# Landmark attention, gated MLP and mish MLP on one core: a new order of steps, other buffers for batch 1, larger weight DMAs

## The chip, the cores and the metric

The kernel runs on one core of a Trainium2 chip. The metric is the device time of one execution in microseconds (us), the median of several runs. In the text PE is TensorE (matrix products, with weight loads, PEld, beside them), DVE is VectorE, ACT is ScalarE, POOL is GpSimd and SP is SyncE, whose queue issues every DMA. PSUM is the memory of 8 banks that PE writes to, SBUF the working memory.

## The reference

Three stages follow each other. With q, k and v of 4 batches, 8 heads, 576 positions and 64 channels:

```python
q_lm = q.reshape(B, H, 32, 18, D).mean(axis=3)
k_lm = k.reshape(B, H, 32, 18, D).mean(axis=3)
A, Bm, C = sm(q, k_lm), sm(q_lm, k_lm), sm(q_lm, k)
Z = Bm.T / (norm(Bm, 1) * norm(Bm, inf) + 1e-06)
for _ in range(6):
    Z = 2 * Z - Z @ Bm @ Z
x = A @ Z @ C @ v                      # 2304 tokens x 512
x = ((x @ w1) * (x @ w2) @ w3) @ w_out # 512 -> 1024 -> 1024 -> 512
h = x @ w_in                           # 512 -> 2048
out = (h * tanh(softplus(h))) @ w_out2 # 2048 -> 512
```

`sm` is a softmax of scaled scores. The weights arrive as 64-bit floats.

## The kernel before

**Order.** The program is a set of named steps, each on one engine, with the steps that must come before it; `ORDER` is a list that says in which order they are issued, written out by hand as one string. Every engine works through its own steps strictly in that order, and `@ACT`, `@POOL` or `@DVE` behind a step picks an engine where there is a choice. A step waits by semaphores for the steps it depends on and for the buffer it takes. Buffers come from small pools and go back when their last reader is done.

**Steps.** In the names, the last figures are batch and the like.
- Weights: `ld` (SP, load a unit of 64-bit words), `da` (L201 on ACT, L203 on DVE), `dm` (L207, DVE), `ds` (L210, ACT) and `db` (L214, DVE) decode a unit to 32 bits in four passes. Units are wo0 to wo7 (w_out), w30 to w315 (w3), wBSC (w1 and w2 for batch pair B, slice S, half C) and x0 on (last stage). `hi` and `lo` split a decoded unit in two parts for the three products of `mm3` (L189 to L191).
- w3 @ w_out: `mm n i` (L356), four for each of the 16 units of w3, two PE instructions each; `ehi` and `elo` bring the sums out. The product is computed once, so that the second and third product of the gated MLP become one.
- Attention of a batch: loads `lk`, `lq`, `lv`; landmark sums `ks`, `qs` (DVE for batch 0, five steps on POOL for the others, L417 to L423); their blocks `bdk`, `bdq`; `as`, `amx`, `asb`, `aex`, `asm`, `aad`, `arc`, `amul`, `atr`, `ahi`, `alo` for A; `cs`, `cm`, `cex`, `cad`, `crc`, `ctr`, `cev`, `cv`, `cve` for C @ v; `bs` to `bp` and `ns` to `npy` for Bm and its norms; six rounds `nm` (PE, L646) and `nu` (DVE, L703) for Z; `lt` and `lte` for Z @ C @ v.
- Landmark products: `m b s` (L850) multiplies Z @ C @ v by slice s of w1 and w2; `mh` and `ml` split the result. `xa` and `xb` multiply it by A, `xc` copies one factor, `xm` (L886) multiplies the two into `hslice`.
- `sh` and `sl` split these, `y` multiplies them by the product of w3 and w_out, `ye` brings it out. Behind the list stands the last stage (`p2`), which is not changed.

**Buffers.** w3 and w_out units are decoded in seven raw buffers, four of the pool `raw` and three of `raw2` (`raw_pool`, L327). The latter lie in the memory of M0 to M2, which the landmark products use later; so `m` waits for `mm 15 3`, the last product of w3 and w_out (`add_m`, L842). q and k of batch 1 lie in W0 and W1 (L242), where w1 and w2 are put later, so the last decode step of their first units waits for batch 1's attention (`add_w12`, L816). H0 to H3 hold the results of `xm` (L240). Of the PSUM banks, two are pool `w`, five `pa` (attention) and one `pb`; the step `widen` (L995) moves two from `pa` to `w` after `mm 15 3`.

Of the kernel before, what the change touches and what calls it, by code (L numbers as in the profile page):

```python
# [7 lines left out]
F32 = mybir.dt.float32  # L8
# [14 lines left out]

ORDER = (
# [127 lines left out]
def kernel(  # L152
# [31 lines left out]
    def words(ap):  # L184
        r, n = ap.shape
        return ap.bitcast(I32).rearrange("r (n w) -> r n w", w=2)

    def mm3(o, lh, ll, rh, rl, first, last):
        T.matmul(out=o, lhsT=lh, rhs=rh, start=first, stop=False)  # L189
        T.matmul(out=o, lhsT=lh, rhs=rl, start=False, stop=False)  # L190
# [55 lines left out]
    M = {}  # L246
# [923 lines left out]
```

## Time and profile before

| | us |
|---|---|
| median of 3 runs (776.62 to 778.1) | 777.49 |
| the profiled execution | 776.88 |
| its span, first to last instruction | 775.1 |
| PE busy in the span | 750.3 |
| DVE busy | 350.4 |
| ACT busy | 337.6 |
| POOL busy | 120.1 |

The profile is of one execution. Busy time of an engine is the time in which one of its instructions ran; matmuls are pipelined, so the mean duration of one can be above the distance between two. An instruction's idle time is that of its engine just before it, with the engine and instruction that ended it. The granted clock is a share of TensorE's full speed.

### The profile page before, as it was taken

Reading aid. Unit: us, or ns where it says so; the run is one execution under the profiler, and the core shown is the slowest. Engines: PE = TensorE matmul, PEld = TensorE weight load, DVE = VectorE, ACT = ScalarE, POOL = GpSimd, SP = SyncE. Lnnn points to the kernel's source line nnn. Section 1 sums busy time; section 2 is a strip of 40 time slices with the busy share of each in tenths; the row PEclk is TensorE's granted clock in tenths of the full one; section 3 lists DMA queues with packets and bytes.
Section 4 is the critical chain, followed back from the end, with each engine's and each line's share of the span. In section 5 each row is a group of like instructions: output and inputs, shape, how many; then the busy total and the mean of one; then the engine's idle time right before and its main releaser. Section 6 shows DMA issues by size and latency. Waiting matters only on the chain.

```text
span 775.1 us, 13036 instructions
## 1 busy us (share of the span) xinstructions
PE 750.3 (97%) x5188; PEld 616.3 (80%) x5188; DVE 350.4 (45%) x706; ACT 337.6 (44%) x737; POOL 120.1 (15%) x120
## 2 busy tenths in 40 slices
PE   6887999999999999999999999999999999999997
PEld 2644457888889889999988888888888888888896
DVE  5878868887886663755165122111111112111111
ACT  5456556666664464876443332222222222222222
POOL 0428100520062413231133200000000000000000
PEclk9989899999999999999999999999999999999999
DMA  8993265742332313434130001000100001000100
GB/s 312 369 329 106 80 192 167 256 127 83 117 114 72 110 55 98 140 117 137 30 107 28 1 0 55 1 0 1 55 0 1 1 0 55 1 0 1 55 1 27
DMA packets 38381, 65.92 MB, mean 85 GB/s; under 512 B 3888, under 2 KB 20400, under 8 KB 38320
## 3 DMA queue, kind: packets, MB, share of 16 engines
q1 hardware_dynamic: 38320, 65.09, 25.3%
q8 instruction: 40, 0.66, 0.3%
q14 instruction: 21, 0.17, 0.1%
HBM read 60.36 MB, written 4.72 MB: 84 GB/s over the span
## 4 chain that ended last, share of the span: by engine, by line
PE 91%; DVE 5%; DMA 2%; issue 1%; ACT 1%; POOL 0%; SPq 0%; DVEq 0%; POOLq 0%
PE ps L189 26%; PE ps L191 26%; PE ps L190 26%; PE ps L356 6%; PE ps L850 2%; PE ps L450 1%; DVE raw L207 1%; DMA raw<-in_wo_dram 1%; PE ps L646 1%; DVE raw L214 1%; PE ps L528 1%; PE ps L587 1%; DMA k<-in_kT_dram 1%; PE ps L566 1%; PE ps L506 0%
## 5 line engine op out<-in xcount | busy, mean ns | idle before, releaser
L1101 ACT ACTIVATE emx<-ps 128x512 f32<-128x512 f32 (+1 forms) x80 | 44.3, 554 | 131.6 <-PE ps L191 131.6
L1103 DVE TENSOR_TENSOR gx<-emx,gx 128x512 fp32r<-128x512 f32 (+1 forms) x40 | 25.6, 639 | 158.6 <-ACT gx L1102 158.6
L189 PE MATMUL ps<-hs,W 128*128 128x288 f32 (+2 forms) x304 | 92.7, 305 | 0.0
L190 PE MATMUL ps<-hs,W 128*128 128x288 f32 (+2 forms) x304 | 92.4, 304 | 0.0
L191 PE MATMUL ps<-hs,W 128*128 128x288 f32 (+2 forms) x304 | 92.2, 303 | 0.0
L207 DVE TENSOR_SCALAR raw<-raw 128x512 uint16<-128x512 uint16 x84 | 74.4, 917 | 37.6 <-ACT raw L201 37.2
L1103 DVE TENSOR_TENSOR hs<-emx,hs 128x512 fp32r<-128x512 f32 (+1 forms) x40 | 25.6, 639 | 136.6 <-ACT hs L1102 136.6
L189 PE MATMUL ps<-AT,M 128*128 128x288 f32 x256 | 78.3, 306 | 1.0 <-DVE M L223 0.9
L190 PE MATMUL ps<-AT,M 128*128 128x288 f32 x256 | 75.6, 295 | 0.0
L191 PE MATMUL ps<-AT,M 128*128 128x288 f32 x256 | 75.5, 295 | 0.0
L210 ACT ACTIVATE raw<-raw 128x512 f32<-128x512 f32 x84 | 55.8, 678 | 29.8 <-DVE raw L207 25.6
L356 PE MATMUL ps<-wo,raw 128*128 128x512 f32 x128 | 61.9, 643 | 5.7 <-DVE raw L214 5.7
L201 ACT ACTIVATE raw<-raw 128x512 int32<-128x512 uint16 x79 | 52.7, 673 | 24.2 <-DMA raw<-in_w_dram 10.5
L190 PEld LDWEIGHTS ps<-hs,W 128*128 128x128 f32 x304 | 57.5, 189 | 1.4
L189 PEld LDWEIGHTS ps<-hs,W 128*128 128x128 f32 x304 | 57.1, 188 | 1.8 <-ACT y L218 0.4
L191 PEld LDWEIGHTS ps<-hs,W 128*128 128x128 f32 x304 | 57.5, 189 | 1.2
L356 PEld LDWEIGHTS ps<-wo,raw 128*128 128x128 f32 x128 | 26.6, 212 | 38.2 <-issue 28.6
L189 PEld LDWEIGHTS ps<-AT,M 128*128 128x128 f32 x256 | 48.1, 188 | 8.2 <-issue 2.1
L1102 ACT ACTIVATE gx<-ps 128x512 fp32r<-128x512 f32 (+1 forms) x40 | 22.2, 556 | 61.2 <-PE ps L190 61.2
L190 PEld LDWEIGHTS ps<-AT,M 128*128 128x128 f32 x256 | 48.1, 188 | 0.0
L191 PEld LDWEIGHTS ps<-AT,M 128*128 128x128 f32 x256 | 48.1, 188 | 0.0
L1102 ACT ACTIVATE hs<-ps 128x512 fp32r<-128x512 f32 (+1 forms) x40 | 22.3, 557 | 54.7 <-PE ps L190 54.7
(219 smaller groups left out, 1652.0 us busy)
## 6 DMA issues: line engine op xcount, KB each, us to landing
raw<-in_w_dram SPq DMA_DIRECT2D x128, 128.0 KB, 2.6
raw<-in_wo_dram SPq DMA_DIRECT2D x22, 512.0 KB, 4.4
raw<-in_w3T_dram SPq DMA_DIRECT2D x32, 256.0 KB, 6.5
raw<-in_wi_dram SPq DMA_DIRECT2D x14, 512.0 KB, 3.9
k<-in_kT_dram SPq DMA_DIRECT2D x8, 576.0 KB, 8.3
q<-in_qT_dram SPq DMA_DIRECT2D x8, 576.0 KB, 9.2
out_dram<-osb SPq DMA_DIRECT2D x18, 256.0 KB, 3.4
vt<-in_v_dram SPq DMA_DIRECT2D x4, 1024.0 KB, 7.5
```

What stands on the lines that cost most here:

```text
L189: T.matmul(out=o, lhsT=lh, rhs=rh, start=first, stop=False)
L190: T.matmul(out=o, lhsT=lh, rhs=rl, start=False, stop=False)
L191: T.matmul(out=o, lhsT=ll, rhs=rh, start=False, stop=last)
L201: S.activation(w[..., 0], q[..., 1], ACTF.Copy, scale=2.0 ** -13, bias=2.0 ** -14 - 0.5)
L207: V.tensor_scalar(q[..., 1], q[..., 3], 0x8000, None, op0=ALU.bitwise_and)
L210: S.activation(f32(w[..., 1]), f32(w[..., 1]), ACTF.Copy, scale=2.0 ** -112)
L214: V.scalar_tensor_tensor(to, w[..., 1], 3, w[..., 0], op0=ALU.logical_shift_left, op1=ALU.bitwise_or)
L356: T.matmul(out=got(f"acc{i}"), lhsT=f32(got(f"w3{n}")[:, o:o + 128, 0]), rhs=WO0[j // 4][:, j % 4], start=j == 0, stop=j == 7)
L850: T.matmul(out=got(f"p{c}{key}")[32 * i:32 * i + 32, 0:256], lhsT=LT[r, b, 2 * c + par, :], rhs=w12(f"w{bp}{s}{c}")[r, par * 256:par * 256 ...
L1101: S.activation(x, zt[n], ACTF.Mish)
L1102: S.activation(gb(n, 0), zt.pop(n), ACTF.Mish)
L1103: V.tensor_tensor(gb(n, 1), x, f32(gb(n, 0)), op=ALU.subtract)
```

## The change

- The order is new from the eighth step on. Batch 0's q comes ahead of its k; batch 1's tensors come after more weights; the rounds of Z of batch 0 come after `mm 7`; batch 2's attention starts ahead of `mm 11`; `widen` comes ahead of `mm 9 1`, `m 0 0` ahead of `mm 15 3`. 16 `da` (w100 to w171) go to DVE and that of wo6 to ACT, `lo` of the last stage's units to DVE in place of POOL, `bdk` and `bdq` of batches 2 and 3 to POOL, six more `sl` to POOL.
- Only four units (the 3rd, 5th, 7th and 10th loaded: w30, wo3, wo4, wo6) use `raw2`; `m` waits for these to be read, in place of `mm 15 3`.
- `widen` waits for `lte1 0` and `alo2 0`, in place of `mm 15 3`.
- q and k of batch 1 lie in H2 and H3, in place of W0 and W1, and H0 to H3 are taken when `xm` first writes them. The decoding of w1 and w2 no longer waits for batch 1's attention.
- A w3 unit is loaded by one DMA in place of two, a unit of w1 and w2 by two in place of four.

```diff
+RAW_M = (3, 5, 7, 10)
...
-    "ld wo0,ld wo1,ld w30,ld wo2,ld wo3,ld w31,ld wo4,lk0 0,lq0 0,lk1 0,lq1 0,lv 0,lk0 1,lq0 1,lk1 1,lq1 1,"
-    "da wo0@ACT,dm wo0,da wo1@ACT,ds wo0,dm wo1,db wo0,ds wo1,da w30@ACT,ld wo5,db wo1,dm w30,da wo2@ACT,ld w32,"
...
-    "as2 1,ks3 2,alo2 0,ks4 2,bmx 1,bsb 1,cs0 1,elo 2,da w314@ACT,qs0 2,elo 3,by 1,bdk0 2@ACT,mm 8 0,bdk1 2@ACT,"
...
+    "ld wo0,ld wo1,ld w30,ld wo2,ld wo3,ld w31,ld wo4,lq0 0,lq1 0,da wo0@ACT,dm wo0,lk0 0,da wo1@ACT,ds wo0,"
+    "dm wo1,db wo0,ds wo1,ld wo5,da w30@ACT,db wo1,dm w30,ld w32,da wo2@ACT,ds w30,dm wo2,lk1 0,da wo3@ACT,db w30,"
...
+    "amul2 0,mm 7 0,ld w310,asm1 1,da w39@ACT,mm 7 1,db w38,npy0 0,mm 7 2,npy1 0,dm w39,mm 7 3,ehi 2,aad0 1,"
+    "arc0 1,ks1 2,ds w39,nm0 0,elo 2,ld w311,cs0 1,da w310@ACT,nu0 0,db w39,ehi 3,mm 8 0,cm00 1,ks2 2,cm10 1,"
...
+    "cv1 1,bsm 1,lte1 0,crc1 1,widen,mm 9 1,bad 1,cve1 1,lv 2,brc 1,qs3 2,da w312@ACT,bml 1,mm 9 2,btr 1,qs4 2,"
...
+    "da w010@ACT,ld w020,m 0 0,dm w010,ehi 6,mm 15 3,mh0 0 0,ks0 3,elo 6,mh1 0 0,atr0 2,ds w010,ml0 0 0,ld w021,"
...
+    "ld w041,asb0 3,da w031@ACT,xm 1 0 0,m 1 1,amx1 3,aex0 3,xa 0 1 0,xm 1 0 1,mh0 1 1,atr1 2,mh1 1 1,asm0 3,"
...
+    def words2(ap):
+        return ap.bitcast(I32).rearrange("(a r) (n w) -> r a n w", a=2, w=2)
...
-    HP = [kept(f"H{i}", [128, NS, HALF], F32, f"h{i}") for i in range(4)]
-    QK1 = {x: kept(f"W{i}", [128, NP, S_LEN], F32, f"{x}1") for i, x in enumerate("qk")}
+    HP = {}
+    QK1 = {x: kept(f"H{i + 2}", [128, NP, S_LEN], F32, f"{x}1") for i, x in enumerate("qk")}
...
-        return "raw2" if len(first) % 7 in (0, 3, 5) else "raw"
+        return "raw2" if len(first) in RAW_M else "raw"
...
-            for a in range(2):
-                nc.sync.dma_start(out=r[:, a * 256:(a + 1) * 256, :],
-                                  in_=words(w3T[r0 + a * 128:r0 + a * 128 + 128, c]))
+            nc.sync.dma_start(out=r.rearrange("p (a n) w -> p a n w", a=2), in_=words2(w3T[r0:r0 + 256, c]))
...
-                for p in range(2):
-                    r0 = (2 * c + p) * 128
-                    nc.sync.dma_start(out=r[:, p, i * 128:(i + 1) * 128, :], in_=words(w[r0:r0 + 128, cols]))
-        after = [f"{x} 1" for x in ("qs4", "as0", "as1", "as2", "ks4", "cs0", "cs1")] if bp == 0 else []
+                nc.sync.dma_start(out=r[:, :, i * 128:(i + 1) * 128, :], in_=words2(w[c * 256:(c + 1) * 256, cols]))
...
-             + ["mm 15 3"] + chain("m", key), mm, {"p0" + key: "w", "p1" + key: "w", key: "M"},
+             + vacated + chain("m", key), mm, {"p0" + key: "w", "p1" + key: "w", key: "M"},
...
+        if u % 4 not in HP:
+            HP[u % 4] = kept(f"H{u % 4}", [128, NS, HALF], F32, f"h{u % 4}")
...
-    step("widen", "none", ["mm 15 3"], lambda e: None, {f"w{i}": "pa" for i in range(2)})
+    in_m = [first[i - 1] for i in RAW_M]
+    vacated = [f"db {u}" for u in in_m] + [f"mm {u[2:]} {i}" for u in in_m if u[1] == "3" for i in range(4)]
+    step("widen", "none", ["lte1 0", "alo2 0"], lambda e: None, {f"w{i}": "pa" for i in range(2)})
```

## Rows read from the trace of the kernel before

**Rows 1.** Busy time by stage of the span (x counts instructions).

```profile
core 0: us, PE busy (x) PEld busy (x) DVE busy (x) ACT busy (x) POOL busy (x), PEclk, DMA share, GB/s
0.00:13.48 13.48, 7.41 (x20) 2.54 (x21) 5.17 (x8) 6.27 (x9) 1.26 (x8) 1.00 0.81 277
13.48:22.32 8.84, 8.84 (x18) 3.98 (x19) 8.48 (x11) 4.66 (x11) 0.00 (x0) 0.81 1.06 382
22.32:43.07 20.75, 13.94 (x267) 10.81 (x266) 18.43 (x44) 10.65 (x30) 11.10 (x9) 0.88 1.05 375
43.07:54.83 11.76, 11.76 (x41) 6.01 (x41) 7.86 (x16) 6.56 (x14) 0.00 (x0) 0.78 1.05 357
54.83:80.06 25.23, 20.34 (x84) 11.26 (x83) 22.59 (x32) 15.12 (x32) 17.96 (x14) 0.91 0.33 101
80.06:110.57 30.51, 30.51 (x93) 13.67 (x96) 20.82 (x55) 14.36 (x31) 2.66 (x3) 0.96 0.44 135
110.57:118.55 7.98, 6.97 (x209) 5.24 (x211) 6.77 (x17) 6.74 (x17) 0.00 (x0) 1.00 0.47 148
118.55:240.00 121.45, 119.26 (x1511) 101.35 (x1508) 96.68 (x242) 76.48 (x198) 32.10 (x39) 1.00 0.45 141
240.00:378.00 138.00, 138.00 (x1144) 132.22 (x1143) 79.24 (x153) 83.38 (x184) 36.54 (x36) 1.00 0.30 100
```

**Rows 2.** Waits of PE, longest in total: us, times, longest.

```profile
PE ps L356 <- DVE raw L214: 5.7, 2, 4.6
PE ps L450 <- DVE AT L223: 4.9, 1, 4.9
PE ps L587 <- ACT et L577: 3.4, 1, 3.4
```

**Rows 3.** Chain of work that ended last, 60 to 120 us: start, length.

```profile
66.85 4.56 DVE raw L207 x3
...
80.13 15.12 PE ps L356 x32
...
96.63 13.94 PE ps L356 x32
```

**Rows 4.** Groups on DVE, 80 to 110 us: busy us, mean ns, idle before.

```profile
L207 DVE TENSOR_SCALAR raw<-raw 128x512 uint16<-128x512 uint16 x7 | 5.2, 742 | 5.4 <-ACT raw L201 5.2
...
L214 DVE SCALAR_TENSOR_TENSOR raw<-raw 128x512 int32<-128x512 int32 x4 | 2.7, 683 | 0.0
```

**Rows 5.** Groups on DVE, 0 to 120 us.

```profile
L223 DVE TENSOR_TENSOR W<-ps,W 128x512 fp32r<-128x512 f32 x8 | 5.4, 687 | 5.5 <-ACT W L218 5.4
...
L537 DVE TENSOR_REDUCE cmx<-ps 128x1 f32<-128x288 f32 x8 | 3.4, 449 | 0.3 <-PE ps L528 0.3
...
L703 DVE SCALAR_TENSOR_TENSOR py<-py,ps 128x128 f32<-128x128 f32 x10 | 2.9, 288 | 1.8 <-PE ps L646 1.7
...
L459 DVE TENSOR_REDUCE mx<-ps 128x16 f32<-128x512 f32 x4 | 2.7, 687 | 0.9 <-PE ps L450 0.9
...
L203 DVE TENSOR_SCALAR raw<-raw 128x512 uint16<-128x512 uint16 x1 | 1.2, 1246 | 0.0
```

**Rows 6.** Groups on DVE, 62 to 77 us.

```profile
L207 DVE TENSOR_SCALAR raw<-raw 128x512 uint16<-128x512 uint16 x6 | 8.0, 1428 | 2.3 <-ACT raw L201 2.3
L214 DVE SCALAR_TENSOR_TENSOR raw<-raw 128x512 int32<-128x512 int32 x5 | 6.7, 1379 | 0.0
```

**Rows 7.** Group of L646 on PE, whole span.

```profile
L646 PE MATMUL ps<-py 32*32 32x64 f32 x320 | 8.7, 225 | 1.3 <-DVE py L703 1.3
```

**Rows 8.** Waits of SP's queue.

```profile
SPq L342 <- PE ps L356: 27.8, 11, 13.2
```

**Rows 9.** DMAs issued 40:60 and 60:80 us: count, size, median us to landing.

```profile
raw<-in_w3T_dram SPq DMA_DIRECT2D x12, 256.0 KB, 5.9
...
raw<-in_w3T_dram SPq DMA_DIRECT2D x6, 256.0 KB, 3.1
```

**Rows 10.** Costliest groups of the page, L201 on ACT.

```profile
L201 ACT ACTIVATE raw<-raw 128x512 int32<-128x512 uint16 x79 | 52.7, 673 | 24.2 <-DMA raw<-in_w_dram 10.5
```

More of the change, by code (lines that the diff above doesn't have):

```diff
@@ L822, in load @@
             for i, w in enumerate((w1, w2)):
-                for p in range(2):
-                    r0 = (2 * c + p) * 128
-                    nc.sync.dma_start(out=r[:, p, i * 128:(i + 1) * 128, :], in_=words(w[r0:r0 + 128, cols]))
-        after = [f"{x} 1" for x in ("qs4", "as0", "as1", "as2", "ks4", "cs0", "cs1")] if bp == 0 else []
-        decode(u, load, lambda: got(u), [], {u: "raw"}, lambda: w12(u), (after, {"f" + u: "w12"}, [u]))
+                nc.sync.dma_start(out=r[:, :, i * 128:(i + 1) * 128, :], in_=words2(w[c * 256:(c + 1) * 256, cols]))
+        decode(u, load, lambda: got(u), [], {u: "raw"}, lambda: w12(u), ([], {"f" + u: "w12"}, [u]))
     def w12(u):
@@ L994 @@
         add_w3(n)
-    step("widen", "none", ["mm 15 3"], lambda e: None, {f"w{i}": "pa" for i in range(2)})
-    moves["widen"] = [(f"w{i}", "w") for i in range(2)]
     for b in range(2):
         attn(b)
+    in_m = [first[i - 1] for i in RAW_M]
+    vacated = [f"db {u}" for u in in_m] + [f"mm {u[2:]} {i}" for u in in_m if u[1] == "3" for i in range(4)]
+    step("widen", "none", ["lte1 0", "alo2 0"], lambda e: None, {f"w{i}": "pa" for i in range(2)})
+    moves["widen"] = [(f"w{i}", "w") for i in range(2)]
     for s in range(NS):
```

236 rows, old and new, of the table ORDER are left out of this document.

## The prediction

> **What bounds the kernel now.** I read the stage windows first, because a share over the whole span would hide where time is lost. The reader should see in them that from 80 us on TensorE (PE) is practically never idle: idle is a row's length less its PE busy time, which gives 0.0 from 80.06 to 110.57, 1.01 up to 118.55, 2.19 in the next 121.45 us and 0.0 up to 378 [rows 1]. No step leaves PE in this change, so nothing can be won there but those few microseconds. Before 80.06 it is otherwise: 6.81 us idle from 22.32 to 43.07 and 4.89 us from 54.83 to 80.06, together 11.70 us, and the granted clock is 0.78 to 0.91 of full, a mixture of the 1.2 and 2.4 GHz levels [rows 1]. Of the 13.48 us ahead of the first product of w3 and w_out, 6.07 are idle too, but the change leaves the first weights where they were.
>
> Then I read who ended PE's waits: decode steps on VectorE (DVE; L214, then L223 behind them) with 5.7 and 4.9 us, and ScalarE's copy L577 with 3.4 [rows 2]. In the two idle stages DVE is busy 18.43 of 20.75 us and 22.59 of 25.23, a share of 0.89 both times: it is the engine that decides there. The chain says the same, with three L207 in 4.56 us, 1.5 us each, before 32 matmuls run behind each other [rows 3]. So the question is how much DVE work stands ahead of PE's early work, and whether DVE gets in the way later.
>
> **Part 1, new order ahead of mm 8 0.** In both orders I counted the steps ahead of mm 8 0 (80.06 us in the trace before).
>
> On DVE's queue 105 become 97. Gone from in front of it are four dm (0.742 each, [rows 4]), two db (0.683, [rows 4]), one da (1.246), one elo (0.687) and five nu (0.288) [rows 5]: 3.0 + 1.4 + 1.2 + 0.7 + 1.4 = 7.7 us. Two amx come in (0.687, [rows 5]), and two asb and two asm, which I put at the same: 4.1 us. A few tiny steps cancel. Net 3.6 us less.
>
> On GpSimd (POOL) 19 become 15, since batch 2's sums come later. That matters to DVE: L207 and L214 took 1.428 and 1.379 us while POOL summed [rows 6], against 0.742 and 0.683 with POOL quiet [rows 4]. Over 6 and 5 instructions that is 7.6 us lost; four of 19 steps fewer make it 1.6 less.
>
> DVE was busy 8.48 + 18.43 + 7.86 + 22.59 = 57.4 us between 13.48 and 80.06 [rows 1]. So 52.2 remain, and the last 3.2 of them (npy0, npy1, dm w39, aad0, arc0, elo 2, nu0, db w39: four by [rows 4, 5], four tiny at 0.2) stand behind db w38, the decode that mm 8 0 needs. 49.0 us at the share 0.89 is 55.1: mm 8 0 starts at 68.6.
>
> PE has eight steps fewer ahead of mm 8 0: five nm of 8.7 / 20 = 0.43 us (16 instructions each, [rows 7]) and lt0, bs and atr2, which I bound by nothing and 0.43 each and put at 0.25: 2.9 us that must be done later. Gain: 80.06 - 68.6 - 2.9 = **8.6 us**. Bounds: with no PE idle at all it would be the 11.7 of above; with DVE's whole 52.2 us at its mean share from 13.48 to 80.06 (57.4 / 66.6 = 0.86) mm 8 0 comes at 74.2, a gain of 3.0. I take the share of the stages in which PE waited, since that is the situation.
>
> The queues that these steps move past: SP now sends batch 0's q and k, wo5 and w32 ahead of batch 1's tensors, at a DMA share around 1.05 until 54.83 [rows 1], so the bytes that mm 2 needs land sooner by what is put behind them. Batch 0's iteration (nm, nu) moves behind mm 7; who waits for it is lt0 0 and then only m 0 0, some 38 us of PE work later. Where this early stall goes: next late is the decode of w3 (rival 1).
>
> **Part 2, landmark products ahead of the end of mm 15.** m 0 0 waits for four early buffers (w30, wo3, wo4, wo6), read last in mm 3, in place of mm 15 3. It can recover the 1.01 us idle before 118.55. The 32 matmuls from 80.13 took 15.12 us, the next 32 took 13.94 at full clock [rows 3], so 1.2 us more come back if PE no longer idles before. Against it stands that widen now comes before mm 9 1: two PSUM banks leave attention some 20 us of PE work earlier, and cs, ctr and lt, which each take two, share three banks. Any wait there holds all PE work behind it. Before, the stretch after widen shows what that costs together with everything else: 2.19 us [rows 1]. So this part lies between 2.2 gained and 2.2 lost; I take **0**.
>
> **Part 3, q and k of batch 1 in H2 and H3.** w1 and w2 no longer wait for batch 1's attention. The added wait is at xm 1 0 0, which must not write H2 before batch 1's sums, scores and c scores have read it. The last of them, cs1 1, stands before mm 8 1, over 50 us of PE work ahead. Cost 0. Were it late, DVE's queue behind it (xm 0 1 0, ml of the next m) and so the next xa would stand.
>
> **Part 4, DMAs.** 16 in place of 32 for w3 and 64 in place of 128 for w1 and w2, with the same bytes. Decoding waited for all pieces of a unit anyway. From 54.83 on the DMA share is 0.33 to 0.47 and SP waits for buffers, not the reverse [rows 1, 8]; before that, the bytes set the pace. 0, with half a microsecond either way for the landing of w30, the first such unit.
>
> **Part 5, other engines.** From m 0 0 to y 2 0, PE's work is about 127 us. There da of 15 units moves from ScalarE to DVE: 15 x 0.742 to 1.246 (the one such da in the trace, [rows 5]) is 11.1 to 18.7 us. Against the stretch of before up to xa 2 2 0, DVE's list has six nu fewer (1.7), six cm and eight sl (0.449 for cm, [rows 5], and an estimate of the same for sl: 6.3), an amx, an asb and an asm (2.1), and 21 tiny ones, an estimate of 0.2 each, under the 0.288 of nu (4.2): 14.3 gone. Three dm and db and two elo come in: 3.5. Before, DVE was busy 96.68 of 121.45 us, 0.80 [rows 1], and 104.7 us up to xa 2 2 0 (14 us more at 79.24 / 138). After: 105.0 to 112.6, a share of 0.83 to 0.89. As PE lost 2.19 us at 0.80, I let that double: **2.2 us lost**. Bounds: nothing, and, if DVE can't be filled beyond 0.80, 112.6 / 0.80 - 127 - 2.2 = 11.6. I take the low end because the early stages show 0.89 to be possible. The 20 lo that go from POOL to DVE fall into the y products, where DVE was busy 0.57 and PE never idle: 0. If that cover went, w_in would be late for the last stage, which starts near 378.
>
> The Trainium skill, "SBUF — State Buffer", section "Who interferes with whom", says that DVE and GpSimd share a port pair that one instruction holds for its whole length: DVE with two SBUF inputs or in a two-port mode waits, and PE and ScalarE never do. The trace agrees (1.428 against 0.742 us), and it speaks against moving da off ScalarE; by the contended price the 15 da would cost 15 x 1.428 = 21.4 us, against the 11.1 to 18.7 above.
>
> **Sum.** 8.6 + 0 + 0 + 0 - 2.2 = 6.4 us. The profiled execution took 776.88 us (span 775.1), so 770.5; the median of the runs, 777.49, is 0.6 above it, which I leave inside the rounding. Forecast 770.5.
>
> **Rivals.**
> (1) The buffers bind. Seven raw buffers take w3 now, four will: the load of w3 unit n+4 waits for mm n 3. From there it is 5.9 us to landing in a busy stretch, 3.1 in a quiet one [rows 9], then da (0.673, [rows 10]), ds as much, dm and db, 2.8 us without queueing; the three mm between give 24 x 0.436 = 10.5 us (13.94 / 32, [rows 3]). That fits by 1.8 to 4.6 us, less than one POOL sum in the way. For it: SP already waited 27.8 us for such buffers [rows 8]. Against: attention's products stand between too. Three rounds (mm 4 to mm 15) of 1.5 us each leave 1.9 of the gain: 775.
> (2) Slower: DVE and POOL lock each other from m 0 0 to y 2 0. 28 dm, 27 db, 15 da and 12 sl stand in DVE's list there, and POOL gets 56 steps in place of 42 (bd blocks and more sl), an estimate of 45 us in place of 36 (32.10 to 240 us, [rows 1], and 14 us more at 36.54 / 138). If half of these 82 pay the 0.69 us between [rows 6] and [rows 4], DVE gets 28 us more, 133 to 141; at 0.89 that is 149 to 158 us for 127 of PE work, and less the gain of 8.6 and the 2.2 idle before, some 12 to 20 us slower: 789 to 797. It decides once the contention passes 14 us: (109 + 14) / 0.89 = 138, 11 over PE's work. For it: the stage at 54.83. Against: there POOL was busy 17.96 of 25.23 us, here about a third. The page's rule names the same lock. If it goes that way only in part, the loss is a few microseconds: 779 to 789.
> (3) Nothing: the early gain turns into waits for banks after widen or for batch 2's and 3's attention, pulled in front of the same DVE. Part 1's low bound 3.0, less 2.2 and a part 2 of -1: 777.
>
> **How the numbers follow.** Forecast 0.54, rival 1 0.21, rival 2 0.16, rival 3 0.09. A difference of 0.2%, 1.6 us, is about what a measurement here can tell from none. Rivals 1 and 2 and the forecast lie on one side of that each, so faster 0.75, same 0.09, slower 0.16. Low end: 11.7 + 2.2 gained and nothing lost would be 763. The high end takes in rivals 1 and 3 up to 778; beyond it rival 2 is left out, and the low end leaves almost nothing.
>
> **What would show it.** Right: mm 8 0 (the 33rd w3 product) starts near 69, the PE idle from 13 to 80 us falls from 11.7 to about 3, DVE's share in the stretch to y 2 0 is 0.83 to 0.89 with PE idle of about 4 us, and L203 takes about 0.8 us. Wrong: PE waiting for DVE's L214 or for DMA of w3 between 45 and 100 us (rival 1), L207, L203 and L214 well over 1 us after 110 (rival 2), or waits of L450, L528 and L566 for banks (rival 3).

## The result, and the profile after

The changed kernel takes 767.27 us, the median of 4 runs (766.28 to 768.29); the kernel before, on the same chip, 777.06 (776.57 to 778.1). The ratio is 0.9872, with a 95% interval from 0.9854 to 0.989: 9.8 us faster, where 7.0 had been forecast against the median (6.4 in the sum). The profiled execution took 767.64 us, its span is 765.9, so 9.2 us less span than before.

The windows by stage of the changed kernel, with the columns of [rows 1]; the cuts are at the first w3 product, at mm 8 0 (the 33rd) and at m 0 0:

```profile
0.00:13.17 13.17, 7.00 (x20) 2.51 (x20) 5.19 (x8) 6.48 (x10) 1.26 (x8) 1.00 0.80 281
13.17:67.50 54.33, 48.56 (x306) 26.39 (x307) 46.62 (x89) 31.89 (x71) 24.79 (x23) 0.97 0.85 301
67.50:117.53 50.03, 50.03 (x609) 25.00 (x610) 33.38 (x107) 21.66 (x61) 7.20 (x13) 1.00 0.38 125
117.53:240.00 122.47, 121.00 (x1360) 104.17 (x1360) 97.77 (x223) 66.47 (x167) 42.28 (x59) 1.00 0.41 130
240.00:378.00 138.00, 138.00 (x1115) 130.66 (x1114) 91.35 (x176) 87.51 (x191) 8.86 (x11) 1.00 0.34 117
378.00:766.00 388.00, 383.99 (x1784) 321.25 (x1782) 82.91 (x133) 107.80 (x208) 15.86 (x10) 1.00 0.05 20
```

And the timeline of PE (start, length, then line and shapes; in brackets the idle time ahead and what ended it). The "..." leave out the other attention products:

```profile
13.17 9.14 PE L360 MATMUL ps<-wo,raw 128*128 128x512 f32 x16 [4.72 <-DVE raw L220]
...
42.23 3.66 PE L360 MATMUL ps<-wo,raw 128*128 128x512 f32 x8
...
56.50 7.14 PE L360 MATMUL ps<-wo,raw 128*128 128x512 f32 x16 [1.33 <-DVE raw L220]
64.84 0.43 PE L650 MATMUL ps<-py 32*32 32x64 f32 x16 [1.20 <-DVE py L691]
65.20 1.19 PE L532 MATMUL ps<-k,bdq 128*64 128x288 f32 x8
67.50 1.13 PE L360 MATMUL ps<-wo,raw 128*128 128x512 f32 x2 [1.11 <-DVE W L229]
68.56 0.43 PE L650 MATMUL ps<-py 32*32 32x64 f32 x16
...
70.04 1.13 PE L360 MATMUL ps<-wo,raw 128*128 128x512 f32 x2
...
117.53 0.66 PE L851 MATMUL ps<-w,LT 64*32 64x256 f32 x16
```

Lines have moved by a few: L360 is the w3 product (L356 before), L213 and L220 are dm and db (L207 and L214), L209 is da on DVE (L203), L229 the copy less its rounded part (L223), L454, L532 and L591 the attention products (L450, L528, L587), L650 and L707 the rounds of Z (L646, L703), L851 is m (L850). In the kernels of the experiments the lines lie lower: the w3 product is mostly L357 there (L353 in e1), dm L210, db L217, da on ScalarE L204.

**Where the 9.2 us come from.** mm 8 0 starts at 67.50 in place of 80.06, 12.56 us earlier, with 2.9 us of PE work, by the prediction's estimate, put behind it: 9.66 gained. Of that 0.31 is the earlier first product (13.17 for 13.48). PE's idle time between the two falls from 11.69 (66.58 less 54.89 busy, the stages of [rows 1]) to 5.77 (54.33 less 48.56): 5.92. The rest, 3.43 by subtraction, is PE work that takes less time: 54.89 less the 2.9 moved is 51.99, and it took 48.56, at a granted clock of 0.97 where the stages before had 0.78 to 0.91. Behind mm 8 0, idle falls from 7.08 to 5.38 us (1.70 gained), of which 3.9 are at the end of either kernel, and the busy time, 693.0, is 2.2 above what 688.0 and the 2.9 moved make. 9.66 + 1.70 - 2.2 = 9.2.

Most of that loss of 2.2 us has a place. Between small products a pair of w3 instructions takes 1.06 us to the next instruction (67.50 to 68.56 above), in a row 13.94 / 16 = 0.87 [rows 3]. There are 15 such lone pairs from 67.5 to 117.53: 15 x 0.19 = 2.9 us, an estimate, less the 1.2 us of slow clock that the 32 products from 80.13 had before. So the w3 products are busy longer in all, at a better clock, as the second of these costliest groups of the page says (before: 61.9 us, mean 643 ns). The first, dm, took 74.4 us at a mean of 917 ns before. POOL is busy 100.2 us in all now, 120.1 before; that dm is shorter because it meets less of POOL fits [rows 4] and [rows 6] but was not tested:

```profile
L213 DVE TENSOR_SCALAR raw<-raw 128x512 uint16<-128x512 uint16 x84 | 66.9, 833 | 29.5 <-ACT raw L207 29.1
...
L360 PE MATMUL ps<-wo,raw 128*128 128x512 f32 x128 | 64.6, 631 | 7.5 <-DVE raw L220 6.0
```

The waits of PE that are left (in total, times, longest) answer to [rows 2]; L450's 4.9 and L587's 3.4 us are gone, and 4.7 of the first row is the start at 13.17:

```profile
PE ps L360 <- DVE raw L220: 6.0, 2, 4.7
PE ps L1048 <- DVE ones L1046: 1.5, 1, 1.5
PE ps L360 <- DVE W L229: 1.4, 2, 1.1
PE ps L195 <- ACT a L224: 1.4, 1, 1.4
PE ps L650 <- DVE py L691: 1.2, 1, 1.2
```

### The profile page after: what moved, and what is told of

Its sections match the earlier page's. It is cut to its first block, busy times and chain, and to the rows that moved or that the text cites. A ratio compares the mean times of both kernels' runs of the same rounds, so it can differ in the third digit from the quotient of the medians.

```text
span 765.9 us, 12838 instructions
## 1 busy us (share of the span) xinstructions
PE 748.6 (98%) x5188; PEld 610.0 (80%) x5188; DVE 357.2 (47%) x735; ACT 321.8 (42%) x705; POOL 100.2 (13%) x123
## 4 chain that ended last, share of the span: by engine, by line
PE 91%; DMA 5%; DVE 2%; ACT 1%; SPq 0%; issue 0%; ACTq 0%
PE ps L195 27%; PE ps L197 26%; PE ps L196 26%; PE ps L360 6%; DMA raw<-in_w3T_dram 3%; PE ps L851 2%; PE ps L454 1%; PE ps L650 1%; DMA raw<-in_w_dram 1%; DMA raw<-in_wo_dram 1%; PE ps L532 1%; PE ps L591 1%; PE ps L510 0%; PE ps L570 0%; DVE raw L213 0%; ACT raw L207 0%
## 5 line engine op out<-in xcount | busy, mean ns | idle before, releaser
L195 PE MATMUL ps<-hs,W 128*128 128x288 f32 (+2 forms) x304 | 92.9, 306 | 0.0
L213 DVE TENSOR_SCALAR raw<-raw 128x512 uint16<-128x512 uint16 x84 | 66.9, 833 | 29.5 <-ACT raw L207 29.1
L195 PE MATMUL ps<-AT,M 128*128 128x288 f32 x256 | 79.0, 309 | 1.5 <-ACT a L224 1.4
L360 PE MATMUL ps<-wo,raw 128*128 128x512 f32 x128 | 64.6, 631 | 7.5 <-DVE raw L220 6.0
L207 ACT ACTIVATE raw<-raw 128x512 int32<-128x512 uint16 x64 | 43.1, 676 | 49.8 <-DMA raw<-in_w3T_dram 15.9
L195 PEld LDWEIGHTS ps<-hs,W 128*128 128x128 f32 x304 | 57.0, 188 | 3.1 <-POOL hs L226 0.8
L195 PEld LDWEIGHTS ps<-AT,M 128*128 128x128 f32 x256 | 48.0, 188 | 11.3 <-issue 2.9
L360 PEld LDWEIGHTS ps<-wo,raw 128*128 128x128 f32 x128 | 23.2, 200 | 29.8 <-issue 16.2
```

The lines of the kernel that those rows point to most:

```text
L207: S.activation(w[..., 0], q[..., 1], ACTF.Copy, scale=2.0 ** -13, bias=2.0 ** -14 - 0.5)
L213: V.tensor_scalar(q[..., 1], q[..., 3], 0x8000, None, op0=ALU.bitwise_and)
L360: T.matmul(out=got(f"acc{i}"), lhsT=f32(got(f"w3{n}")[:, o:o + 128, 0]), rhs=WO0[j // 4][:, j % 4], start=j == 0, stop=j == 7)
```

## The experiments

Every kernel ran beside the kernel before on its own chip; ratios are to that. e5 is the changed kernel once more.

| kernel | us (lowest to highest) | ratio |
|---|---|---|
| e1, order alone | 767.24 (766.69 to 768.5) | 0.9892 [0.9873, 0.9911] |
| e2, DMAs and place of q, k alone | 773.64 (771.84 to 775.35) | 0.9966 [0.9951, 0.9981] |
| e12, DMAs alone | 774.11 (772.02 to 774.96) | 0.9964 [0.995, 0.9979] |
| e4, rounds of Z put back early | 772.34 (771.65 to 774.37) | 0.9959 [0.9946, 0.9971] |
| e3 and e11, m held | 766.86 and 767.79 (766.68 to 769.56) | 0.9891 [0.987, 0.9912], 0.9899 [0.9876, 0.9922] |
| e5, changed kernel again | 767.89 (766.56 to 769.67) | 0.9867 [0.9845, 0.9889] |
| e6, da back on ScalarE | 767.31 (767.17 to 769.79) | 0.9869 [0.9845, 0.9893] |
| e10, split DMAs | 769.06 (767.2 to 769.97) | 0.9878 [0.9856, 0.9899] |
| e7, other loads | 768.6 (766.59 to 768.87) | 0.9869 [0.985, 0.9889] |
| e8, elo 2 early | 766.56 (765.89 to 766.79) | 0.9878 [0.9854, 0.9902] |
| e9, both | 765.98 (765.33 to 767.2) | 0.9875 [0.9853, 0.9897] |

**e1, the new order alone,** with the buffers and DMAs of before; m waits for mm 15 3, so that step moves ahead of m 0 0. The first pair of lines is against the changed kernel's order, the second against the kernel before:

```diff
-m 0 0,dm w010,ehi 6,mm 15 3,
+mm 15 3,m 0 0,dm w010,ehi 6,
...
-    step("widen", "none", ["mm 15 3"],
+    step("widen", "none", ["lte1 0", "alo2 0"],
```

> The kernel before with the new order and the early widen alone: old DMAs, old buffers (q and k of batch 1 in W0 and W1, seven raw buffers throughout), m held by mm 15 3 (so m 0 0 stands one product later). If the order makes the gain (my theory), it is within 1.5 us of the changed kernel, 766 to 769, and the 33rd product starts between 66 and 69 us. If the buffers or the larger DMAs are needed, most of the 9.8 us is missing: 771 to 777.

Measured 767.24, 8.5 us under its own runs of before (775.73). The order carries nearly the whole gain. In e1's timeline of PE, mm 6 0 and mm 8 0 (the 33rd product) stand nearly where they do in the changed kernel, with all seven raw buffers:

```profile
55.87 7.14 PE L353 MATMUL ps<-wo,raw 128*128 128x512 f32 x16 [0.50 <-DVE raw L211]
...
66.86 1.13 PE L353 MATMUL ps<-wo,raw 128*128 128x512 f32 x2 [1.11 <-DVE W L220]
```

**e2, the code without the order,** and **e12, the DMAs without the place of q and k.** e12's edit is the first two of these, e2 has all (with the last, w1 and w2 are decoded without waiting for batch 1, and H0 to H3 are taken late):

```diff
-            for a in range(2):
-                nc.sync.dma_start(out=r[:, a * 256:(a + 1) * 256, :],
-                                  in_=words(w3T[r0 + a * 128:r0 + a * 128 + 128, c]))
+            nc.sync.dma_start(out=r.rearrange("p (a n) w -> p a n w", a=2), in_=words2(w3T[r0:r0 + 256, c]))
...
-                for p in range(2):
...
+                nc.sync.dma_start(out=r[:, :, i * 128:(i + 1) * 128, :], in_=words2(w[c * 256:(c + 1) * 256, cols]))
...
-    QK1 = {x: kept(f"W{i}", [128, NP, S_LEN], F32, f"{x}1") for i, x in enumerate("qk")}
+    QK1 = {x: kept(f"H{i + 2}", [128, NP, S_LEN], F32, f"{x}1") for i, x in enumerate("qk")}
```

> The reverse: the old order, with one DMA per w3 unit, two per unit of w1 and w2, and q and k of batch 1 in H2 and H3. My theory: nothing, 776 to 778. If SP's queue or the waits of w1 and w2 for batch 1 cost anything: 774 or less. If a larger DMA lands later at the start: 778 to 780.

> The kernel before with the fewer, larger weight DMAs alone: its order, its buffers, q and k of batch 1 in W0 and W1 as they were. With both the DMAs and the new place of q and k, in the old order, the time was 773.64 us, a ratio of 0.9966 [0.9951, 0.9981], where the prediction had 0 for either. Theory A (the DMAs do it, since the first w3 unit, w30, lands sooner and so mm 0 0 starts sooner): the ratio is again 0.996 to 0.997, and the decode of w30 starts near 9 us in place of 10.25. Theory B (the place of q and k does it, since the decoding of the first w1 and w2 units no longer waits for batch 1's attention): the ratio is 0.999 to 1.001, as the prediction had for the DMAs.

Both gain the same: e2 2.1 us (773.64 for 775.73), where I had expected nothing, and e12 2.0 (774.11 for 776.12). So it is the DMAs, and the place of q and k adds nothing that shows. In the timeline of ScalarE, before and then e12, the da of w30 starts at 10.25 and at 8.68 us, since the unit lands sooner:

```profile
10.25 0.65 ACT L201 ACTIVATE raw<-raw 128x512 int32<-128x512 uint16 x1 [1.78 <-DMA raw<-in_w3T_dram]
```

```profile
8.68 0.66 ACT L204 ACTIVATE raw<-raw 128x512 int32<-128x512 uint16 x1 [0.38 <-DMA raw<-in_w3T_dram]
```

e12's first w3 product and the 33rd, in the timeline of PE, are 1.17 and 1.78 us ahead of 13.48 and 80.06:

```profile
12.31 8.84 PE L357 MATMUL ps<-wo,raw 128*128 128x512 f32 x16 [4.08 <-DVE raw L217]
...
78.28 15.44 PE L357 MATMUL ps<-wo,raw 128*128 128x512 f32 x32
```

**e4, batch 0's norms and rounds back early** in the changed kernel, all in a row ahead of mm 3 0:

```diff
-da w35@ACT,mm 3 0,...,ds w37,nc 0,mm 5 2,...,npy0 0,mm 7 2,npy1 0,...,nm0 0,elo 2,...,nu5 0,aex2 1,
+da w35@ACT,nc 0,ntr 0,nx 0,nml 0,nad 0,nrc 0,npy0 0,npy1 0,nm0 0,nu0 0,...,nm5 0,nu5 0,mm 3 0,...
```

> The changed kernel with batch 0's norms and six rounds (nc to nu5) put back ahead of mm 3 0. My theory (DVE's list ahead of early PE work decides): 14 DVE steps of 3.9 us come ahead of mm 3, PE waits for the rounds, and mm 8 0 starts 2 to 5 us later at 2.2 us more PE work done: 768 to 771. If the rounds could stand anywhere (the loads or the clock decide): 766.5 to 768. If rounds behind mm 7 only cost, because each lone product between two rounds takes PE longer: 764 to 766.

Measured 772.34, 5.5 us over e3 on the same chip and above the 768 to 771 that I had expected. The timeline of PE shows the price:

```profile
44.73 0.65 PE L647 MATMUL ps<-py 32*32 32x64 f32 x16 [3.58 <-DVE py L688]
45.79 0.65 PE L647 MATMUL ps<-py 32*32 32x64 f32 x16 [0.41 <-DVE py L704]
...
50.40 5.11 PE L357 MATMUL ps<-wo,raw 128*128 128x512 f32 x8
```

And the windows of e4 for the rounds and for mm 3:

```profile
44.70:50.40 5.70, 3.61 (x96) 2.35 (x97) 1.44 (x5) 0.00 (x0) 0.00 (x0) 0.50 0.64 195
50.40:55.50 5.10, 5.10 (x16) 2.10 (x10) 3.90 (x10) 1.29 (x2) 2.67 (x3) 0.72 0.31 106
```

3.58 us for npy, five times 0.41 between the rounds, and mm 3 in 5.11 us in place of 3.66, at a granted clock of 0.50 in the rounds and 0.72 in mm 3 where the changed kernel has 1.00: 3.58 + 2.05 + 1.45 = 7.1, less the 1.20 that nm0 waits at 64.84 in the changed kernel, 5.9. In the rounds DVE is busy only 1.44 of 5.70 us: PE and DVE wait for each other.

This is the price of rounds in a row, and not the share of the rounds in Part 1. In the kernel before they stood early too, but between other attention products, and PE waited for them 2.1 us in the whole span:

```profile
PE ps L646 <- DVE py L703: 2.1, 5, 0.5
```

**e3 and e11, m held by mm 15 3 and widen behind it** (one kernel, run twice); elo 4 and elo 5 come right behind their ehi, since attention keeps its banks longer.

```diff
-             + vacated + chain("m", key), mm,
+             + ["mm 15 3"] + chain("m", key), mm,
...
-    step("widen", "none", ["lte1 0", "alo2 0"],
+    step("widen", "none", ["mm 15 3"],
```

> The changed kernel with m 0 0 held by mm 15 3 again, and widen behind mm 15 3 (elo 4 and elo 5 come right behind their ehi, since the sums of mm 12 need their banks). My theory: part 2 is worth nothing, 766.5 to 769, as m 0 0 was only one product ahead. If landmark products ahead of mm 15's end are what wins, or two more banks for the sums: 770 to 774. If three banks for attention cost waits: below 766.

> The changed kernel with m 0 0 held until mm 15 3 ends, once more, beside the two kernels above. If the hold costs nothing, 766.5 to 768.5 as it was; if the other order of elo 4 and elo 5 in it gains, it is under both of the others by over 0.5 us.

766.86 and 767.79 against 767.27 and 767.89 without the hold: no difference in these times. By the ratios, each to the kernel before on its own chip, the hold stands 0.002 to 0.003 higher (0.9891 and 0.9899 against 0.9872 and 0.9867), with intervals that overlap: a cost of some two microseconds is not excluded.

**e5 and e6, the changed kernel again, and with the 16 da back on ScalarE.**

```diff
-da w100@DVE
+da w100@ACT
...
```

> The changed kernel itself, as the measure for the other kernels of this job: 765.5 to 768, a ratio to the kernel before of 0.986 to 0.990.

> The changed kernel with the 16 da of w100 to w171 back on ScalarE. Part 5 of the prediction let them cost up to 2.2 us; the trace after shows 1.5 us of PE idle in that stretch, so by my theory the most there is to win is 1.5: within 1 us of the changed kernel. If DVE still holds PE in a way that the idle time does not show: over 1.5 us faster. If ScalarE's queue is the tighter one there (copies of xc and mh behind a da that waits for its load): 1 to 4 us slower, with PE waiting for L224.

Windows of 120 to 260 us, the changed kernel and then e6:

```profile
120.00:260.00 140.00, 138.53 (x1505) 121.48 (x1505) 110.40 (x245) 71.83 (x179) 47.34 (x68) 1.00 0.40 127
```

```profile
120.00:260.00 140.00, 138.46 (x1501) 121.13 (x1501) 99.59 (x231) 80.52 (x194) 44.88 (x68) 1.00 0.41 126
```

DVE loses 10.8 us of work and PE's busy time stays (138.53 and 138.46 of 140): 767.31 against e5's 767.89, no difference. These da cost nothing where they are.

**e10, split DMAs in the changed kernel** (the reverse of e12's edit).

> The changed kernel with the DMAs of before (two per w3 unit, four per unit of w1 and w2). Part 4 of the prediction: nothing, within 0.7 us. After the old order with larger DMAs came out 2 us faster than the kernel before, the rival: the first w3 unit lands 0.5 to 1.5 us sooner as one DMA, and splitting costs 1 to 2 us, all of it ahead of 13 us.

769.06 against e5's 767.89, with da of w30 at 9.71 (e5: 9.08) and the first product at 12.97 (12.39). The ranges overlap, and the first profile of the changed kernel has 9.74 and 13.17, no sooner than e10: by this pair they are not told apart. All the traces of the new order together point the same way as e12. With split DMAs (e1 and e10) the first product starts at 13.08 and 12.97; with the larger ones it starts between 11.81 and 12.64 in eight of nine profiles, and at 13.17 in one.

**e7, the loads of w36 and w37 ahead of batch 2's k and q; e8, elo 2 right behind ehi 2; e9, both.** These go for two of the three waits, those at 56.50 and 67.50.

```diff
-da wo6@ACT,lk0 2,cm01 0,...,bmx 0,lk1 2,bsb 0,...,as0 1,lq0 2,asb2 0,lq1 2,...,ld w36,...,ld w37,
+da wo6@ACT,cm01 0,...,bmx 0,bsb 0,...,as0 1,asb2 0,...,ld w36,lk0 2,lk1 2,...,ld w37,lq0 2,lq1 2,
...
-ehi 2,aad0 1,arc0 1,ks1 2,ds w39,nm0 0,elo 2,
+ehi 2,elo 2,aad0 1,arc0 1,ks1 2,ds w39,nm0 0,
```

> The changed kernel with batch 2's loads moved: k behind the load of w36, q behind that of w37. Rival 1 in its milder form (the loads of w3 come too late behind 2.4 MB that POOL needs 15 us later): w36 lands some 4 us sooner, the 1.3 us of PE idle ahead of mm 6 goes, and 1 to 2 us are won. If DVE and POOL set the pace up to mm 8 0 anyway, the idle time only moves to the products behind it: within 0.7 us. If batch 2's sums now come late: slower by 1 us or more.

> The changed kernel with one edit: `elo 2` stands right behind `ehi 2` in the order instead of where the order puts it late; in the changed kernel it came on VectorE at 66.8 us, and its W held mm 8 0 for 1.1 us (the wait at 67.50 on W). Theory A (that wait is an idle stretch of TensorE on the path, and nothing else is late there): the wait of 1.1 us goes, mm 8 0 starts at about 66.4 less what the start of mm 0 0 moves, and the time is about 1 us under the changed kernel, 766.3. Theory B (VectorE is the engine that is late at 56 to 67, so the copy only moves forward in its list): the wait of 1.2 us for py ahead of nm 0 0, or the one of 1.3 us for raw ahead of mm 6 0, grows by what the copy takes, 0.6 us or so, and the time stays within 0.5 us of the changed kernel's 767.3 to 767.9.

> The changed kernel with `elo 2` right behind `ehi 2` and with lk 2 and lq 2 behind the loads of w36 and w37. If the three idle stretches of TensorE at 56 to 67.5 us (1.3, 1.2 and 1.1 us) each have a cause of their own, two of the three go and the time is 1.5 to 2 us under the changed kernel, 765.5 to 766. If VectorE's list sets the pace of that stretch, the idle time ahead of the 33rd w3 product stays about 3 us in sum and the time is within 0.5 us of the changed kernel's.

In the changed kernel the chain of waits leads from mm 3 over a load to the wait at 56.50:

```profile
42.40 3.51 PE ps L360 x8
45.90 0.02 issue
45.92 7.93 DMA raw<-in_w3T_dram
53.85 0.02 issue
53.88 0.68 ACT raw L207
```

The load goes out when mm 3's last product has read its buffer, and lands 7.93 us later. e7 gains nothing, 768.6 against e5's 767.89. ScalarE has w36 at 48.40 in it, over 4 us earlier than the 52.58 of the changed kernel, and yet the wait of mm 6 0 is 2.06 us. The timeline of DVE in e7 says why:

```profile
49.98 0.73 DVE L210 TENSOR_SCALAR raw<-raw 128x512 uint16<-128x512 uint16 x1
54.09 1.12 DVE L210 TENSOR_SCALAR raw<-raw 128x512 uint16<-128x512 uint16 x1 [3.38 <-ACT raw L204]
...
55.27 1.40 DVE L217 SCALAR_TENSOR_TENSOR raw<-raw 128x512 int32<-128x512 int32 x2
```

The order has dm w36, dm w37, db w36, db w37. dm w36 is done at 50.7, but db w36, for which mm 6 0 waits, stands behind dm w37, and w37 lands at 53.4 us here and at 53.85 in the changed kernel. Putting db w36 ahead of dm w37 was not tried. The wait also costs clock. Of mm 6 and mm 7, e8 (idle 0.49 ahead, granted clock 1.00) and e9 (2.49 ahead, granted clock 0.81), in the timeline of PE:

```profile
55.53 7.14 PE L357 MATMUL ps<-wo,raw 128*128 128x512 f32 x16 [0.49 <-DVE raw L217]
...
65.38 1.13 PE L357 MATMUL ps<-wo,raw 128*128 128x512 f32 x2
```

```profile
55.82 8.83 PE L357 MATMUL ps<-wo,raw 128*128 128x512 f32 x16 [2.49 <-DVE raw L217]
```

In e8 the wait on W ahead of mm 8 0 is gone, and from the first w3 product to mm 8 0 it takes 53.06 us (12.32 to 65.38) in place of 54.33 and, in e5, 54.34. Its runs lie under e11's on the same chip with no overlap, and e9's median, 765.98, is the lowest of all; but their ratios, 0.9878 and 0.9875, are not below the changed kernel's. That they beat it is not shown.

## Why the prediction was right, point by point

**The bound** was named rightly: PE's early waits for DVE. From 67.5 to 117.53 PE isn't idle at all, and the order alone gives 8.5 us (e1).

**Part 1** was forecast at 8.6, mm 8 0 at 68.6; it came at 67.50, a gain of 9.7. The size was near in part by luck. 49.0 us of DVE work at a share of 0.89 were 46.6 at 0.86, and these errors nearly cancel. By the idle sign, 11.7 falling to about 3, idle time alone should have given 8.7 us; it fell to 5.8 and gave 5.9. What made up for it was missing from the sum: the clock, which I let return only in the 32 products behind mm 8 0 (1.2 us), rose ahead of it too, where PE's work got 3.4 us shorter. The price of lone products, 2.9 us by the estimate above, was missing on the other side. Nor does DVE's share of busy time say all: in e4's rounds it is 0.25 (1.44 of 5.70), and PE waits all the same. Which of the moved steps gave how much of e1's 8.5 us was not tested.

**Part 2** at 0: e3 and e11 agree, within about two microseconds. The 1.01 us idle ahead of 118.55 went, and no wait for banks came: L454, L532 and L570 have 0.4 us or less each in the waits of PE.

**Part 3** at 0: e2 and e12 differ by 0.0002 in ratio.

**Part 4** at 0, with half a microsecond for the landing of w30, was mis-sized. In the old order the DMAs give 0.36%, 0.21 to 0.5, some 2 us by the medians (e12), of which 1.17 is in the trace ahead of the first product. "The bytes set the pace" held on the whole, not for the first unit, which DVE and PE were waiting for. In the new order it is about 1 us that can be seen (e10), inside the noise. By ratio, e1 and e12 would make 0.9892 x 0.9964 = 0.9856 together, and the changed kernel has 0.9872: they add up within their intervals.

**Part 5**, 2.2 us lost, is the step that failed. DVE's share from m 0 0 to 240 us is 97.77 / 122.47 = 0.80, under the 0.83 to 0.89 forecast, and PE's idle time there is 1.47, not 4: before it was 2.19 [rows 1]. Nearly all of it is one wait of 1.4 us, L195 for ScalarE's `a`. Up to y 2 0, at 246.91, DVE is busy 102.51 of 129.38 us, so its work too is under the 105.0 to 112.6 forecast. The fault is in "as PE lost 2.19 us at 0.80, I let that double": the idle time did not follow DVE's share. e6 takes 10.8 us of DVE's work away, and PE's idle time from 120 to 260 us is 1.54 in place of 1.47. What the change did lose behind mm 8 0 is 2.2 us by longer PE work, by the estimate above mostly lone products, against 1.70 us of idle time gained: 0.5 in all. So of the 2.8 us by which the sum was low (6.4 for 9.2), 1.1 lie ahead of mm 8 0 and 1.7 behind it. L209 took 0.828 us, near the low end of its bounds. The groups on DVE from 118 to 222 us (busy us, mean ns):

```profile
L213 DVE TENSOR_SCALAR raw<-raw 128x512 uint16<-128x512 uint16 x22 | 16.2, 807 | 2.6 <-ACT raw L207 2.6
L220 DVE SCALAR_TENSOR_TENSOR w<-raw 128x512 int32<-128x512 int32 x21 | 14.9, 728 | 1.3 <-ACT raw L216 0.9
...
L209 DVE TENSOR_SCALAR raw<-raw 128x512 uint16<-128x512 uint16 x9 | 7.2, 828 | 1.0 <-DMA raw<-in_w_dram 1.0
```

**Rival 2** is refuted by these rows. POOL was about as busy as it foresaw (45.51 us up to y 2 0, for an estimate of 45), but against the quiet 742 and 683 ns [rows 4] L213 and L220 pay 65 and 45 ns: 22 x 0.065 + 21 x 0.045 = 2.4 us for about half of its 82 instructions, where 28 were foreseen for all.

**Rival 1** was right that the load behind the wait at 56.50 goes out only when mm 3 frees its buffer, and wrong in the price: one wait, of 1.33 us here and 0.50 in e5, not three of 1.5. As far as these traces show, the buffers don't make even that: e1, which keeps all seven, also waits 0.50 us there, and its decode of w37 starts at 53.18 us, between 52.64 in e5 and 53.88 here. e7 shows that the order of decode steps holds the place.

**Rival 3** did not come: what moved forward was covered.

## What to carry to other kernels

Count a serial loop between two engines (here rounds of PE work with 0.41 us of waiting in between) by what PE could do meanwhile, and put it between products that are ready: in a row, with the norms ahead of them, the rounds cost 5.5 us in e4, though DVE was busy for only a quarter of them. When a stall goes, ask what the clock gives back, too: here 3.4 us beside 5.9 us of idle time. And don't scale idle time with an engine's share of busy time; look for the wait that makes it, since 10.8 us of DVE work came and went here with no effect on the time.

## What the runs showed of the hardware that was not expected

**Lone large products.** A pair of 512-column products takes 1.06 us from its start to the next instruction's when it stands between small ones, 0.87 in a row of 32. In stretches of 4 and 10 products the time to the next instruction is 1.92 us (from 79.59) and 4.50 (from 81.76), 0.18 and 0.14 more than in the long row: the extra comes once for each stretch, not for each product. The trace does not say why.

**Clock after a short stall.** e5 and the first timeline of the changed kernel are of one kernel. Both wait 1.2 us for nm0 and 1.11 for mm 8 0, yet the pair at mm 8 0 took 1.13 us in one and 1.96 in the other, where the granted clock is 0.60 up to 71 us, mostly the lower level, 1.2 GHz. In e1, e3, e10 and e11, with the same two waits, it took 1.13. Timeline of PE and windows of e5:

```profile
66.73 1.96 PE L360 MATMUL ps<-wo,raw 128*128 128x512 f32 x2 [1.11 <-DVE W L229]
...
70.85 1.13 PE L360 MATMUL ps<-wo,raw 128*128 128x512 f32 x2
```

```profile
64.00:66.70 2.70, 1.55 (x24) 0.75 (x24) 2.67 (x6) 1.72 (x3) 2.52 (x4) 1.00 0.55 188
66.70:71.00 4.30, 4.27 (x27) 1.68 (x28) 3.89 (x11) 2.27 (x6) 3.78 (x10) 0.60 0.01 4
```

To the next w3 product it is 4.12 us (66.73 to 70.85) in place of 2.54 (67.50 to 70.04), so the same stall of 1.1 us can cost 1.6 more.

**A long wait inside an instruction.** While POOL summed q, one L691 on DVE, 128 x 64 elements from two inputs in SBUF, took 2.27 us; the one just before it, with an input from PSUM, 0.21. Timeline of DVE and then of POOL in the changed kernel:

```profile
62.39 0.21 DVE L691 TENSOR_TENSOR py<-ps,cc 128x64 f32<-128x64 f32 x1
62.52 2.27 DVE L691 TENSOR_TENSOR py<-bm,cc 128x64 f32<-128x64 f32 x1
```

```profile
61.99 2.71 POOL L421 TENSOR_TENSOR tree<-q 128x1152 f32<-128x1152 f32 x1
```

It ends at 64.79, right behind POOL's step at 64.70, and nm0 at 64.84 waits for it. The Trainium skill, "SBUF — State Buffer", section "Who interferes with whom", says that a DVE instruction with two SBUF inputs contends with a GpSimd instruction that reads SBUF, and that the order of issue decides which of the two is blocked. The trace agrees: POOL's step had started 0.53 us earlier. This one wait for the lock that rival 2 feared cost PE 1.2 us, in a stage that rival 2 did not speak of.
